# Ordering the stores of plain weights behind the TensorE instruction issued ahead of them

## The chip, the cores and the metric

The kernel runs on one core of a Trainium2 chip. The metric is the device time of one execution in microseconds (us); lower is better. The engines are TensorE (PE in the profile), VectorE (DVE), ScalarE (ACT), GpSimd (POOL) and SyncE (SP), which here does little but issue DMAs.

## The reference

Attention over pooled keys, then a gated feed-forward network, all in float32:

```
# q, k, v: (8 batches, 8 heads, 576 tokens, 64)
k_p = k.reshape(B, H, 72, 8, D).mean(axis=3)      # v_p likewise
scores = q @ k_p.T / sqrt(64)
attn = exp(scores - max) / (sum + 1e-9)
x = (attn @ v_p) -> 4608 tokens x 512
h = x @ w_in                                       # 512 x 2048
g = h * clip(h + 3, 0, 6) / 6
out = g @ w_out                                    # 2048 x 512
```

## The kernel before, in words

**Numbers.** A float32 operand is split into a high and a low part of TensorE's short type, and each product is made as high·high + high·low + low·high: three matmuls for one. `w_in` and `w_out` lie in SBUF as such pairs.

**Blocks of tokens.** The 4608 tokens are cut into blocks of 512, 256 and ten times 384. Blocks 0 to 3 are "plain". For each of 16 slices f of the hidden dimension a step makes h (L841, PE), relu (L849, ACT), the gate g (L853, DVE), its high part ghi (L857, ACT) and low part glo (L861, DVE); the second product out (L872, PE) follows two steps later. The finished sums go through ACT (L877) to DRAM by SP (L878). Blocks 4 to 11 are taken two at a time as four "super-blocks". There a 2x2 product is made of seven products of sums and differences (L1134 for the first matrix, L1188 and L1261 for the second), and the weights for these stream back from DRAM.

**Attention.** It goes in small pieces between the matmuls of the block ahead: loads of q, k and v (`qt` L241, `kst` L249, `vst` L284 and L288), scores (L463, PE), maximum (L467, DVE), exponential (L472, ACT), sums and reciprocals (`sm`, L489 and L490, DVE), scaling (`a`, L501, POOL), transposes (L572, L574, PE) with copies (L583, L585, L596, L598), and the product with v (L646, PE). The pooling of v is at L383 on DVE.

**Weights to DRAM.** During blocks 2 and 3, hooks that run after a step write what the super-blocks will stream:

- `sums_of` (L930 to L948), 16 rounds, at every even step of blocks 2 and 3: DVE adds two pairs of weight quarters into the tile `wq` (L939) and mixes them (L944, four times), ACT casts the high part (L945), DVE subtracts for the low part (L946), and SP stores four pieces of 128 KB (L948). The tile `wq` exists once, so a round's first addition must wait for the landing of the stores of the round before.
- `plain_of` and `store` (L950 to L962), 32 hooks with 56 stores of 256 KB in all (L951): weights as they are, straight from the tiles `w`, into the DRAM tensors `wd` (first matrix) and `w2d` (second). One hook follows each step of block 2, two follow each of the first eight steps of block 3.
- `swap`, after step 9 of block 3, gives half of the weight tiles back and opens the first pool of the weight stream; `chunk` (L980 to L994) then loads tiles of 512 KB (L992), four in the first pool (`wsFalse`) and three in the second (`wsTrue`). The second pool opens when block 3 ends. Its first tile lies where `wq` lay, so its load waits until the last round's four stores have landed.

**What sets the order.** Each engine has one queue and takes it in order; SP's queue holds every load and store. Up to step 3 of block 1 the order is a table written by hand (`ORDER`, applied by `put_in_order`). From there on a scheduler builds each engine's queue from the order of the source, its estimates, and the dependencies. `behind(ins, name)` (L166) adds one such dependency: the instruction stands behind the one named in the schedule. It adds no semaphore, so on the chip nothing waits for it. `traced` is the list of all instructions issued so far in the source. A DMA has one of eight semaphores in turn, so it also waits for the landing of the one eight before it.

Numbers behind an underscore are the program's names of buffers: `wq_3755`, `wq_3832` and `wq_3910` are the last three rounds of `sums_of`; `qt_1902` is a tile of q for block 2; `wsTrue_4002` is the first tile of the second weight pool.

Of the kernel before, what the change touches and what calls it, by code (L numbers as in the profile page):

```python
# [98 lines left out]
def attention_moe_kernel(  # L99
# [66 lines left out]
    def behind(ins, name):  # L166
        no_sync = mybir.DependencyInfo(mybir.DependencyClass.NoSync, mybir.DependencyReason.DATA)
        tc.add_manual_dep(ins, name, no_sync, reason="order")

    traced = nc.cur_bb.bb.instructions  # L170
# [778 lines left out]

    def store(to, src):  # L950
        nc.sync.dma_start(to, src)  # L951

    def plain_of(i, n):
        if n < 2:
            for o, (r, q) in list(RAW.items())[2 * n : 2 * n + 2]:
                store(dram_of(i, o), pair_of(i)[r][:, :, q])
        else:
            f = 2 * i + n - 2
            for m in range(2):
                w = w_of[f, 1][:, m].bitcast(F32).rearrange("p (q c) -> p q c", q=2)  # L960
                store(w2_dram[f // 4][:, f % 4, :, m], w)
# [605 lines left out]
```

## Time and profile before

| what | value |
|---|---|
| median of 3 runs | 894.1 us (892.81 to 894.3) |
| the profiled execution's own time | 893.88 us |
| its span, first to last instruction | 892.1 us |
| PE busy | 869.2 us, 97% of the span |
| DVE, ACT, POOL busy | 75%, 62%, 9% |
| granted TensorE clock | 1.00 throughout |
| DMA traffic | 200 MB, mean 224 GB/s |
| the chain of work that ended last | PE 80%, DVE 8%, DMA 5%, ACT 4% |

How to read the profile. A row of a timeline has the start, the length, the engine, the source line, the operation, output<-input, the shape and a count of instructions put together; in brackets stands the idle time of that engine ahead of the row and what ended it. A row of the windows has a stretch of time, and for each engine its busy time in it with its count of instructions; then the granted clock, the share of the DMA engines' time in use, and GB/s. "SPq" rows are issues of DMAs by SP; how long the transfer itself takes is told apart, as the time from issue to landing.

### The profile page before, as it was taken

The page shows a single profiled execution, that of the slowest core. Times are in us where ns is not written, and L with a number is a line of the kernel's source. Part 1 is how long each engine was busy: PE and PEld are TensorE (multiplying, and loading weights), DVE is VectorE, ACT ScalarE, POOL GpSimd, SP SyncE. Part 2 cuts the span into 40 slices and gives each one's busy share as a digit, 9 for nine tenths or more (in the row PEclk, how much of TensorE's full clock was granted, in tenths as well). Part 3 has the DMA queues.
Part 4 walks back from the last instruction along what each step waited for, and adds up shares of the span by engine and source line. Part 5 has one row for each costly group of instructions (what it writes and reads, how often), then busy time and mean ns, then how long its engine had stood idle before and what let it go on. Part 6 is the DMA issues. An engine that isn't in the chain of part 4 may idle for free.

```text
span 892.1 us, 15646 instructions
## 1 busy us (share of the span) xinstructions
PE 869.2 (97%) x5360; PEld 812.3 (91%) x5360; DVE 665.9 (75%) x1340; ACT 553.6 (62%) x1515; POOL 83.6 (9%) x168
## 2 busy tenths in 40 slices
PE   7899999999999999999999999999999999999998
PEld 6788888988989998998888999999999999999998
DVE  6999864567877785869788688897597877466664
ACT  5998766655656655778344688665577746355442
POOL 4100002110211100102000101100100200000000
PEclk9999999999999999999999999999999999999999
DMA  9970205995425234996587968877976777877873
GB/s 294 392 293 1 72 24 192 360 327 167 130 67 160 71 129 135 368 315 225 180 271 239 383 218 295 265 239 236 331 250 213 226 233 240 275 253 238 266 264 132
DMA packets 124654, 200.00 MB, mean 224 GB/s; under 512 B 13216, under 2 KB 81056, under 8 KB 124576
## 3 DMA queue, kind: packets, MB, share of 16 engines
q1 hardware_dynamic: 124432, 199.00, 67.8%
q8 instruction: 43, 0.70, 0.3%
q14 instruction: 35, 0.29, 0.1%
q10 hardware_dynamic: 144, 0.00, 0.0%
HBM read 158.08 MB, written 40.89 MB: 223 GB/s over the span
## 4 chain that ended last, share of the span: by engine, by line
PE 80%; DVE 8%; DMA 5%; ACT 4%; issue 2%; SPq 1%; POOL 0%; DVEq 0%; ACTq 0%; POOLq 0%
PE psx L1134 22%; PE psx L1261 19%; PE pso L872 12%; PE psh L841 12%; PE psx L1188 7%; PE psa L646 3%; PE psa L463 3%; ACT e L472 2%; PE psa L572 1%; DMA raw<-w_in_l 1%; DMA raw<-w_out_l 1%; DMA wd<-wq 1%; DVE vst L383 1%; DMA wsFalse<-wd 1%; DVE wq L939 1%
## 5 line engine op out<-in xcount | busy, mean ns | idle before, releaser
L1134 PE MATMUL psx<-x,wsFalse 128*128 128x384 f32 x768 | 151.8, 341 | 1.7 <-DVE g L1098 0.8
L841 PE MATMUL psh<-xhi,w 128*128 128x384 f32 (+2 forms) x520 | 145.9, 340 | 0.5 <-DVE g L853 0.4
L1134 PEld LDWEIGHTS psx<-x,wsFalse 128*128 128x128 f32 x768 | 133.6, 188 | 3.2 <-ACT c L1107 1.3
L1113 ACT CAST part<-g 128x768 fp32r<-128x768 f32 x100 | 83.3, 836 | 85.0 <-PE psx L1261 65.8
L1115 DVE TENSOR_TENSOR part<-g,part 128x768 fp32r<-128x768 f32 x100 | 95.2, 955 | 46.5 <-ACT part L1113 46.1
L872 PE MATMUL pso<-w,ghi 128*128 128x512 f32 x384 | 120.7, 398 | 0.4 <-ACT o L877 0.4
L1134 PE MATMUL psx<-x,wsTrue 128*128 128x384 f32 x576 | 115.8, 342 | 2.4 <-DMA wsTrue<-wd 2.3
L1261 PE MATMUL psx<-wsFalse,part 128*128 128x256 f32 x864 | 108.3, 282 | 1.5 <-DVE part L1115 1.1
L1261 PEld LDWEIGHTS psx<-wsFalse,part 128*128 128x128 f32 x864 | 105.2, 189 | 2.3 <-DVE part L1115 1.3
L1134 PEld LDWEIGHTS psx<-x,wsTrue 128*128 128x128 f32 x576 | 99.6, 188 | 3.1 <-DVE g L1092 3.1
L841 PEld LDWEIGHTS psh<-xhi,w 128*128 128x128 f32 x520 | 93.2, 188 | 8.2 <-DVE g L853 1.1
L472 ACT ACTIVATE e<-psa,mx 128x72 f32<-128x72 f32 x256 | 78.6, 324 | 23.7 <-DVE mx L467 22.4
L841 PE MATMUL psh<-xlo,w 128*128 128x384 f32 (+2 forms) x260 | 87.1, 336 | 0.0
L501 POOL TENSOR_TENSOR a<-e,sm 128x256 f32<-128x256 f32 x60 | 41.0, 683 | 478.3 <-DVE sm L490 377.9
L1261 PE MATMUL psx<-wsTrue,part 128*128 128x256 f32 x648 | 81.3, 283 | 0.0
L1261 PEld LDWEIGHTS psx<-wsTrue,part 128*128 128x128 f32 x648 | 79.3, 191 | 0.2 <-DVE part L1115 0.2
L872 PEld LDWEIGHTS pso<-w,ghi 128*128 128x128 f32 x384 | 69.1, 188 | 11.2 <-ACT o L877 0.7
L1090 ACT ACTIVATE r<-g,small 128x384 f32<-128x384 f32 x96 | 58.8, 621 | 28.4 <-DVE g L1098 28.0
L872 PE MATMUL pso<-w,glo 128*128 128x512 f32 x192 | 74.4, 399 | 0.0
L1098 DVE TENSOR_TENSOR g<-psx,c 128x384 f32<-128x384 f32 x96 | 52.3, 553 | 28.7 <-PE psx L1134 20.6
L1107 ACT COPY c<-psx 128x384 f32<-128x384 f32 x96 | 45.0, 485 | 28.5 <-PE psx L1134 28.1
L1092 DVE SCALAR_TENSOR_TENSOR g<-r,g 128x384 f32<-128x384 f32 x96 | 54.5, 576 | 9.7 <-ACT r L1090 9.2
(139 smaller groups left out, 1473.2 us busy)
## 6 DMA issues: line engine op xcount, KB each, us to landing
wsFalse<-wd SPq DMA_DIRECT2D x64, 512.0 KB, 4.6
wsTrue<-wd SPq DMA_DIRECT2D x48, 512.0 KB, 4.9
wsFalse<-w2d SPq DMA_DIRECT2D x31, 512.0 KB, 5.0
wsFalse<-w2t SPq DMA_DIRECT2D x27, 512.0 KB, 5.0
wsTrue<-w2d SPq DMA_DIRECT2D x21, 512.0 KB, 5.0
wsTrue<-w2t SPq DMA_DIRECT2D x21, 512.0 KB, 4.9
raw<-w_in_l SPq DMA_DIRECT2D x16, 512.0 KB, 8.6
raw<-w_out_l SPq DMA_DIRECT2D x16, 512.0 KB, 9.2
```

The costliest lines, as they stand in the source:

```text
L472: nc.scalar.activation(self.e[:, h], self.ps[:, h], AF.Exp, bias=self.mx[:, h : h + 1], accum_out=self.sm[:, h : h + 1])
L841: nc.tensor.matmul(self.ps, l[f][:, c, :], r[:, c, :], start=c == 0 and i == 0, stop=c == NCC - 1 and i == 2)
L872: nc.tensor.matmul(pos, l, r, start=f == 0 and i == 0, stop=f == NF - 1 and i == 2)
L1090: nc.scalar.activation(r, src, AF.Relu, bias=half_low, scale=GSCALE / (6.0 * WSCALE))
L1092: nc.vector.scalar_tensor_tensor(out=g_of[i][:, k], in0=r, scalar=GSCALE, in1=src, op0=ALU.min, op1=ALU.mult)
L1098: nc.vector.tensor_tensor(out=g_of[i][:, k], in0=ps, in1=kept, op=ALU.add)
L1107: nc.scalar.copy(c, ps)
L1113: nc.scalar.copy(t[:, 0], src)
L1115: nc.vector.tensor_tensor(out=t[:, 1], in0=src, in1=t[:, 0].bitcast(F32), op=ALU.subtract)
L1134: nc.tensor.matmul(ps, w[:, l, c * P : (c + 1) * P], t[:, r, c], start=o in (1, 2, 5) and c == 0 and k == 0, stop=c == 1 and k == 2, skip_ ...
L1188: nc.tensor.matmul(to, l, w[:, qs, r], start=f == 0 and k == 0, stop=end and k == 2)
L1261: nc.tensor.matmul(to, t[:, l, k, i * P : (i + 1) * P], w[:, k, r], start=begin and k == 0 and y == 0 and i % 2 == 0, stop=m == NM - 1 and ...
```

## The change

One line is added to `store`, the function that issues the 56 plain stores:

```diff
     def store(to, src):
         nc.sync.dma_start(to, src)
+        behind(traced[-1], next(i for i in reversed(traced) if i.engine == mybir.EngineType.PE).name)
```

Each store is placed behind the last PE instruction issued ahead of it in the source: as a rule an `out` matmul (L872) of the step whose hook it is, in a block's first two steps, which have none, a matmul of h (L841). As this enters a schedule, it moves rows on every engine. Lines behind L952 have numbers higher by one after it (L992 becomes L993).

The order is the same on each engine up to about the 610th row of PE, in block 1, and again from the second half of the first super-block. Three places in between matter.

**SP, at the end of block 1.** `wd` and `w2d` are the DRAM tensors of plain weights, `w_...` tiles of weights. Before, from the last early load of k to the load of qt_1902 (rows left out at the line of dots):

```order
L249 DMA kst_1647<-k_l 128x576
L951 DMA wd0_92<-w_0_344 128x2x256 x2
L951 DMA wd5_97<-w_1_486 128x2x256
L951 DMA w2d0_120<-w_0_431 128x2x256 x2
L241 DMA qt_1837<-q_l 128x4x128
...
L951 DMA wd22_114<-w_11_1049 128x2x256
L951 DMA w2d2_122<-w_10_1006 128x2x256 x2
L241 DMA qt_1902<-q_l 128x4x128
L951 DMA w2d2_122<-w_11_1049 128x2x256 x2
```

After, from the same load of k:

```order
L249 DMA kst_1647<-k_l 128x576
L241 DMA qt_1837<-q_l 128x4x128
L284 DMA vst_1839<-v_l 128x2x256
L284 DMA vst_1861<-v_l 128x2x256
L284 DMA vst_1904<-v_l 128x2x256
L284 DMA vst_1957<-v_l 128x2x256
L241 DMA qt_1902<-q_l 128x4x128
L241 DMA qt_2026<-q_l 128x4x128
L288 DMA vst_2028<-vr_l 32x2x256 x3
L249 DMA kst_2032<-k_l 128x576
L241 DMA qt_2450<-q_l 128x4x64
L951 DMA wd0_92<-w_0_344 128x2x256 x2
```

The loads of q, v and k for block 2 have moved ahead of the first plain store; the stores follow later, among other rows.

**DVE, the last rounds of `sums_of`, at the end of block 3.** `g` and `glo` are the steps' gate and low part, `mx` and `sm` the softmax's. Before:

```order
L946 TENSOR_TENSOR wq_3755<-wq_3755 128x512
L861 TENSOR_TENSOR glo_3821<-g_3816,ghi_3819 128x384
L853 SCALAR_TENSOR_TENSOR g_3861<-g_3861,psh_3848 128x384
L861 TENSOR_TENSOR glo_3866<-g_3861,ghi_3864 128x384
L939 TENSOR_TENSOR wq_3832<-w_14_1196 128x256
L939 TENSOR_TENSOR wq_3832<-w_15_1212 128x256
L853 SCALAR_TENSOR_TENSOR g_3894<-g_3894,psh_3881 128x384
...
L946 TENSOR_TENSOR wq_3832<-wq_3832 128x512
L853 SCALAR_TENSOR_TENSOR g_3942<-g_3942,psh_3929 128x384
L861 TENSOR_TENSOR glo_3947<-g_3942,ghi_3945 128x384
L467 TENSOR_REDUCE mx_4011<-psa_4013 128x4
L467 TENSOR_REDUCE mx_4038<-psa_4040 128x4
L939 TENSOR_TENSOR wq_3910<-w_14_1196 128x256
```

After:

```order
L853 SCALAR_TENSOR_TENSOR g_3894<-g_3894,psh_3881 128x384
L946 TENSOR_TENSOR wq_3755<-wq_3755 128x512
L861 TENSOR_TENSOR glo_3899<-g_3894,ghi_3897 128x384
L853 SCALAR_TENSOR_TENSOR g_3942<-g_3942,psh_3929 128x384
L939 TENSOR_TENSOR wq_3832<-w_14_1196 128x256
L939 TENSOR_TENSOR wq_3832<-w_15_1212 128x256
L861 TENSOR_TENSOR glo_3947<-g_3942,ghi_3945 128x384
...
L490 RECIPROCAL sm_4012<-sm_4012 128x4
L946 TENSOR_TENSOR wq_3832<-wq_3832 128x512
L939 TENSOR_TENSOR wq_3910<-w_14_1196 128x256
L939 TENSOR_TENSOR wq_3910<-w_15_1212 128x256
L944 TENSOR_TENSOR wq_3910<-wq_3910 128x128 x4
L946 TENSOR_TENSOR wq_3910<-wq_3910 128x512
```

Each round has moved back against the steps' gates: L946 of wq_3755 stood behind the gate g_3816 and now stands behind g_3894, two steps later, and the first additions of wq_3910 now stand directly behind L946 of wq_3832.

**SP, at the same place.** `out` are finished results, `ws` tiles of the weight stream. Before:

```order
L878 DMA out<-o_3977 128x512
L948 DMA wd27_119<-wq_3910 128x2x128
L948 DMA wd26_118<-wq_3910 128x2x128
L948 DMA wd25_117<-wq_3910 128x2x128 x2
L878 DMA out<-o_3983 128x512
L878 DMA out<-o_3989 128x512
L992 DMA wsFalse_4101<-wd7_99 128x1024
L992 DMA wsTrue_4002<-wd4_96 128x1024
```

After:

```order
L878 DMA out<-o_3977 128x512
L878 DMA out<-o_3983 128x512
L878 DMA out<-o_3989 128x512
L993 DMA wsFalse_4101<-wd7_99 128x1024
L948 DMA wd27_119<-wq_3910 128x2x128
L948 DMA wd26_118<-wq_3910 128x2x128
L948 DMA wd25_117<-wq_3910 128x2x128 x2
L993 DMA wsTrue_4002<-wd4_96 128x1024
```

The last round's stores stand behind two more outputs and a load of the weight stream, and directly ahead of the load that waits for them.

## The prediction

> **What bounds the kernel now.** I read the page first: is there one engine that everything waits for?
>
> ```profile
> span 892.1 us, 15646 instructions
> PE 869.2 (97%) x5360; PEld 812.3 (91%) x5360; DVE 665.9 (75%) x1340; ACT 553.6 (62%) x1515; POOL 83.6 (9%) x168
> ```
>
> TensorE (PE) works for 869.2 of 892.1 us. The change adds no arithmetic, so it can only touch the 23 us in which PE stands idle, or make new idle time. The profiled run took 893.88 us, its span and 1.78 us around it. My sum is made on 893.88; the median of the three runs shown is 894.1, 0.2 us higher, which I neglect. A measurement of this kernel tells about 0.2% from no change, 1.8 us; faster means below 892.1, slower above 895.7.
>
> Next, the instruction that is edited: the source view of L951, the plain stores.
>
> ```profile
> L951 SPq DMA_DIRECT2D w2d<-w x32: 428/724/1452, 149.9 to 198.1; - x32
> L951 SPq DMA_DIRECT2D wd<-w x24: 426/720/1174, 148.1 to 192.5; - x24
> its engine sat idle before it (us, times) until:
> who waited for it (us, times):
> busy tenths in 40 slices 0000000000000000000000000000000000000000
> DMA to landing us min/median/max: 3.0/4.7/6.6
> ```
>
> All 56 stores leave SP's queue as one burst between 148.1 and 198.7 us, and the list of who waited for them is empty: when they land is of no interest to anybody. What matters is what stands behind them and what is reordered around them. The order of the changed kernel agrees with before's on every engine up to about 178 us and again from about 450 us, so I read only that stretch: PE's idle time by windows, then each engine's timeline where a window has some.
>
> ```profile
> core 0: us, PE busy (x) PEld busy (x) DVE busy (x) ACT busy (x) POOL busy (x), PEclk, DMA share, GB/s
> 186.00:203.00 17.00, 15.39 (x85) 13.29 (x83) 10.58 (x30) 8.24 (x33) 2.35 (x5) 1.00 1.00 320
> 203.00:345.00 142.00, 141.30 (x759) 128.46 (x760) 108.46 (x273) 83.06 (x260) 15.80 (x29) 1.00 0.40 115
> 358.00:450.00 92.00, 89.99 (x507) 84.22 (x508) 74.23 (x175) 62.79 (x201) 12.13 (x24) 1.00 0.79 267
> 450.00:892.10 442.10, 434.44 (x2958) 422.28 (x2957) 324.67 (x568) 251.75 (x610) 26.78 (x52) 1.00 0.77 254
> ```
>
> PE misses 1.61 us in 186–203, 0.70 in 203–345, 2.01 in 358–450 and 7.66 in the common tail; the DMA engines are full (share 1.00) in the first of these. The granted clock is 1.00 in every row.
>
> **Part 1, removed: the crowd at 190–203 us.** Six rows of PE, with SP's, DVE's and ACT's row that lead to them:
>
> ```profile
> 183.54 0.55 SPq L241 DMA_DIRECT2D qt<-q_l  x1
> ...
> 191.09 0.46 DVE L467 TENSOR_REDUCE mx<-psa 128x4 f32<-128x288 f32 x1 [4.29 <-PE psa L463]
> ...
> 191.64 0.32 ACT L472 ACTIVATE e<-psa,mx 128x72 f32<-128x72 f32 x1 [5.64 <-DVE mx L467]
> ...
> 193.06 0.41 PE L572 MATMUL psa<-ident,a 128*128 128x128 f32 x2 [0.19 <-issue]
> 194.28 0.44 PE L572 MATMUL psa<-ident,a 128*128 128x128 f32 x2 [0.70 <-POOL a L501]
> 198.08 0.44 PE L646 MATMUL psa<-ahi,vhi 128*128 128x384 f32 x1 [0.25 <-DVE alo L585]
> 198.54 0.34 PE L646 MATMUL psa<-ahi,vlo 128*128 128x384 f32 x1
> 198.98 0.44 PE L841 MATMUL psh<-xhi,w 128*128 128x384 f32 x1
> 202.95 0.74 PE L872 MATMUL pso<-w,ghi 128*128 128x512 f32 x2 [0.36 <-ACT o L877]
> ```
>
> The load of qt_1902 stands behind 40 of the stores and leaves at 183.54. Its scores are therefore late; DVE sits idle for 4.29 us and ACT for 5.64 before them, and then scores, softmax, transposes and the first steps of block 2 all come at once. PE breaks five times: 0.19, 0.70, 0.25, 0.10 (198.98 less the end of the matmul before, 198.54 + 0.34) and 0.36, together 1.60 us, which is the window's 1.61. A break costs a little more than its idle row says, because matmuls overlap. I take that from the 36 in a row at 349.87 (quoted below): 6.50 us less one matmul's 0.34, over 35, is a pitch of 0.176, so a matmul of 0.34 hides 0.16 under its neighbour. Five times 0.16 is 0.8, and the crowd costs 2.4 us.
>
> In the changed order qt_1837, four vst, qt_1902 and qt_2026 come ahead of all 56 stores in SP's queue, and PE takes the scores of qt_1902 inside step 14 of block 1, before 186 us. DVE's and ACT's idle stretches get filled, and the crowd is gone. I put the saving at **2.4** us; at least 0, since ACT's part of the last break (an output's copy, 0.36) doesn't hang on the load, and other work may crowd instead.
>
> **Part 2, removed: two small breaks.**
>
> ```profile
> 248.04 0.35 PE L646 MATMUL psa<-ahi,vhi 128*128 128x192 f32 x1 [0.31 <-DVE alo L585]
> ...
> 256.54 0.44 PE L841 MATMUL psh<-xhi,w 128*128 128x384 f32 x1 [0.39 <-DVE g L853]
> ```
>
> These two are all of the 0.70 us of 203–345; with 0.16 each they cost 1.0. In the changed order DVE does no sums (L939) between the low halves that the first waits for. I take half, **0.5**, with 0 and 1.0 as ends. The stores themselves now lie between 187 and about 300 us, in a stretch with a DMA share of 0.40; nobody waits for their landing, so I charge nothing. The first reader, the weight stream's first tiles, comes at about 318 us, and without that cover each store would cost its 4.7 us of landing once.
>
> **Part 3, moved: the sums of weights at the end of block 3.** The tile wq exists once, so a round of it is a ring through three queues: DVE L939, L944, ACT L945, DVE L946, four stores on SP, their landing, then the next round's L939. DVE's waits for a landing (9.8 us in 7 times) and the ring's last two rounds:
>
> ```profile
> DVE wq L939 <- DMA wd<-wq: 9.8, 7, 3.3
> ...
> 338.09 0.55 DVE L853 SCALAR_TENSOR_TENSOR g<-g,psh 128x384 f32<-128x384 f32 x1 [1.09 <-ACT g L849]
> ...
> 340.86 0.69 DVE L946 TENSOR_TENSOR wq<-wq 128x512 fp32r<-128x512 f32 x1 [0.69 <-ACT wq L945]
> 342.34 0.55 DVE L853 SCALAR_TENSOR_TENSOR g<-g,psh 128x384 f32<-128x384 f32 x1 [0.79 <-ACT g L849]
> ...
> 345.12 0.76 DVE L939 TENSOR_TENSOR wq<-w 128x256 f32<-128x256 f32 x2 [0.35 <-DMA wd<-wq]
> ...
> 346.37 1.25 DVE L944 TENSOR_TENSOR wq<-wq 128x128 f32<-128x128 f32 x3
> 348.35 0.69 DVE L946 TENSOR_TENSOR wq<-wq 128x512 fp32r<-128x512 f32 x1 [0.73 <-ACT wq L945]
> ...
> 347.70 0.62 ACT L945 CAST wq<-wq 128x512 fp32r<-128x512 f32 x1 [1.89 <-issue]
> ...
> 341.58 1.96 SPq L948 DMA_DIRECT2D wd<-wq  x4
> 349.52 2.00 SPq L948 DMA_DIRECT2D wd<-wq  x4
> 352.64 0.40 SPq L992 DMA_DIRECT2D wsFalse<-wd  x1
> 353.22 0.82 SPq L992 DMA_DIRECT2D wsTrue<-wd  x2
> ...
> 353.22 5.34 DMA wsTrue<-wd
> ...
> 349.87 6.50 PE L1134 MATMUL psx<-x,wsFalse 128*128 128x384 f32 x36
> 358.70 1.47 PE L1134 MATMUL psx<-x,wsTrue 128*128 128x384 f32 x7 [2.34 <-DMA wsTrue<-wd]
> ```
>
> From issue of a round's first store to the next L939 it is 345.12 − 341.58 = 3.5 us. The first load of the second weight pool, wsTrue_4002, takes the place of wq in SBUF, so SP holds it until the last round's stores have landed: 349.52 + 3.5 = 353.0, issue 353.22, 5.34 us on the way, and PE stands for 2.34 before 358.70. So **this ring already sets the end of block 3**; every us by which it gets later, PE gets later.
>
> In the changed order the ring runs up to two steps of the block behind. Followed in before's clock: L946 of wq_3755 stands behind the g at 338.09, so it ends at 338.09 + 0.55 + 0.69 = 339.3; its stores have landed 3.5 later, at 342.8. L939 of wq_3832 stands behind the g at 342.34 (before: ahead of 338.09), so from 342.9. To the end of L946 of wq_3832 its own work and what stands between (glo, two mx, sm) are about 0.76 + 0.55 + 0.81 + 1.25 + 0.62 + 0.69 = 4.7, so 347.6. Stores, landing: 351.1, where L946 waits for nothing else. Then L939 of wq_3910: 0.76 + 1.25 + 0.62 + 0.69 with 0.1 of handover is 3.4, so 354.5 for the stores (before 349.52, **5.0 later**). The three outputs and wsFalse_4101, ahead of them now, are due by 352.64 and don't hold them. Landing 358.0, issue of wsTrue_4002 358.2.
>
> ```profile
> wsTrue<-wd SPq DMA_DIRECT2D x48, 512.0 KB, 4.9
> ```
>
> With the median of 4.9 it lands at 363.1, and PE goes on 0.13 later (358.70 − 353.22 − 5.34 = 0.14). One group of six matmuls, psx_3999<-x7_3958, has moved from ahead of this wait to behind it: 6 × 0.176 = 1.05. PE's place that was reached at 358.70 is reached at 363.2 + 1.05 = 364.3: **5.5 us later**. Ends: if the next L939 is held only by the four stores' issue (2.0) instead of 3.5, twice, it is 2.5; with the 5.34 us of the first load and 1.5 more of DVE's other work it is 7.5. What stands behind DVE's wait for the landing at 351.1 is the first group's g (L1098, L1099 after); PE's next groups wait for it and for ACT's copies behind L945, but only until about 357, inside the wait that is there anyway.
>
> [...]
>
> **Sum.** 893.88 − 2.4 − 0.5 + 5.5 = 896.5; the tail is ordered as before.
>
> **The rivals.**
>
> *The pause is paid back (no change).* While PE waits 5.5 us, DVE, ACT and SP go ahead with attention work that PE later stands for: 2.01 us in 358–450. Speaks for it: those waits are for that work. Against: DVE is itself held up at 351–355. If all come back: 896.5 − 2.0 = 894.5. Chance 0.28.
>
> *The ring is no later (faster).* The one place is the landing of wq_3910's stores. If the rounds catch up because L939 of wq_3832 and of wq_3910 find their landings done, wsTrue_4002 leaves as at 353.2 and only the moved group is paid: 893.88 − 2.9 + 1.05 = 892.0, and 890.5 with the second part whole and the group hidden. It decides at a landing of wsTrue_4002 at 358.7 in before's clock. Against it: L939 of wq_3910 stands directly behind L946 of wq_3832 and needs its landing, with 3.5 us between. [...] Chance 0.13.
>
> *A new crowd on top (slower still).* Behind the late ring DVE has L1098's, the part sums and vst pooling of the first super-block, all 5 us late; if PE must stand for them once more by 2–3 us, 899. Chance 0.09.
>
> *It does nothing.* The added line is an order only, with no semaphore; the changed order moves hundreds of rows, so: 893.9, chance 0.01.
>
> **How the numbers follow.** The forecast's own case has 0.49, with 894.5 to 898.5 from the ends of part 3 beside the full gains. Faster is the second rival, 0.13; the same holds the first rival, the last one, and a little of the forecast's lower end, 0.32; slower is the rest, 0.55. For 8 in 10 the range reaches into the faster case, to 891.3, and into the crowd, to 899.3.
>
> **What would show it.** Right: L951 from about 187 to 300 us; DVE's 4.29 and ACT's 5.64 gone and 186–203 with PE idle under 0.4; the last L948 issued about 5 us later, relative to PE, and PE's row at wsTrue with 7 us of idle or near it. Wrong: wsTrue_4002's wait still at 2.3, or breaks elsewhere in 203–345 over 1 us.

## The result, and the profile after

The changed kernel takes 906.37 us (median of 4 runs, 904.69 to 908.16), before on the same chip 893.45 (891.7 to 894.3). The ratio is 1.0147, 95% interval 1.0122 to 1.0173: slower by 12.9 us, where 2.6 were forecast. The profiled execution took 908.16 us, 14.28 more than the profiled one of before. Of the runs below, one execution of e10 (2714 us) and one of e11 (954 us) lie far above their fellows and are left out of the ratios.

Page of after, the first line and the engines' busy time:

```profile
span 906.3 us, 15649 instructions
PE 876.4 (97%) x5360; PEld 818.3 (90%) x5360; DVE 665.5 (73%) x1340; ACT 555.1 (61%) x1515; POOL 83.4 (9%) x168
```

PE does the same 5360 matmuls in 7.2 us more of busy time, which a later order can't do by waiting alone: part of the loss is a slower clock (0.83 and 0.74 granted in two of the windows below). The source view of L951, the stores of plain weights:

```profile
L951 SPq DMA_DIRECT2D w2d<-w x32: 359/542/1188, 188.2 to 300.9; - x32
L951 SPq DMA_DIRECT2D wd<-w x24: 434/508/765, 186.5 to 298.1; - x24
who waited for it (us, times):
```

They lie where they were forecast, and still nobody is named as waiting for them. Windows of after, then of before (its rows for 186–203 and 203–345 stand in the prediction):

```profile
186.00:203.00 17.00, 17.00 (x95) 16.09 (x94) 10.79 (x31) 8.67 (x26) 1.15 (x3) 1.00 0.54 170
203.00:300.00 97.00, 96.66 (x532) 87.54 (x530) 70.23 (x195) 57.96 (x207) 13.61 (x27) 1.00 0.75 232
300.00:345.00 45.00, 42.25 (x213) 37.88 (x214) 35.17 (x76) 24.22 (x55) 0.99 (x2) 1.00 0.39 122
345.00:365.00 20.00, 15.16 (x67) 14.14 (x66) 8.27 (x20) 8.42 (x23) 2.18 (x4) 0.83 0.72 235
365.00:420.00 55.00, 55.00 (x334) 54.41 (x333) 45.69 (x110) 44.82 (x155) 9.06 (x18) 1.00 0.90 297
420.00:440.00 20.00, 15.43 (x62) 13.14 (x61) 15.11 (x41) 9.00 (x31) 2.97 (x4) 0.74 0.43 137
```

```profile
300.00:345.00 45.00, 45.00 (x233) 40.82 (x232) 35.03 (x73) 24.06 (x52) 1.85 (x4) 1.00 0.34 106
345.00:365.00 20.00, 17.66 (x102) 16.85 (x101) 11.31 (x28) 12.16 (x34) 1.78 (x4) 1.00 0.78 259
365.00:420.00 55.00, 53.93 (x328) 53.07 (x327) 45.62 (x117) 44.13 (x156) 8.55 (x18) 1.00 0.89 301
420.00:440.00 20.00, 19.76 (x100) 16.57 (x100) 15.37 (x35) 10.73 (x33) 3.58 (x6) 1.00 0.54 171
```

PE is without a break in 186–203 now. It loses in three places: 2.75 us of idle time in 300–345; 4.84 in 345–365, where before has 2.34, with a granted clock of 0.83; and 4.57 in 420–440, before 0.24, at 0.74. Matmul by matmul, after stands to before (in before's clock) so:

| place in before, us | 180 | 300 | 331 | 345 | 364 | 378 | 423 | 499 | end |
|---|---|---|---|---|---|---|---|---|---|
| after later by, us | -1.7 | -5.0 | -1.6 | -1.5 | +4.5 | +4.5 | +10.2 | +12.2 | +14.3 |

The -1.7 at 180 and the +2.1 behind 499 lie where the two orders are the same; I take them for the scatter of single executions. What lies between is 13.9, and the difference of the medians is 12.9.

**300–345.** Timeline rows of after, PE, DVE and SP:

```profile
301.15 0.41 PE L646 MATMUL psa<-ahi,vhi 128*128 128x384 f32 x1 [1.19 <-ACT ghi L857]
324.57 0.44 PE L841 MATMUL psh<-xhi,w 128*128 128x384 f32 x1 [1.22 <-DVE g L853]
...
298.62 0.76 DVE L939 TENSOR_TENSOR wq<-w 128x256 f32<-128x256 f32 x2 [1.61 <-DMA wd<-wq]
316.34 0.76 DVE L939 TENSOR_TENSOR wq<-w 128x256 f32<-128x256 f32 x2 [1.97 <-DMA wd<-wq]
323.97 0.55 DVE L853 SCALAR_TENSOR_TENSOR g<-g,psh 128x384 f32<-128x384 f32 x1
...
284.93 2.66 SPq L951 DMA_DIRECT2D w2d<-w  x4
293.67 2.06 SPq L948 DMA_DIRECT2D wd<-wq  x4
298.61 3.00 SPq L951 DMA_DIRECT2D w2d<-w  x4
```

The stores of block 3 now stand between the rounds of `wq` in SP's queue. DVE waits longer for the landing of a round, and the gates that PE needs (g, L853) are queued behind that wait. At 324 they are not directly behind it: from the end of the wait at 316.34 to the gate at 323.97 DVE works without a pause, mostly on the super-block's sums (L1039 and L1047, seven rows). DVE's list of waits in 200–345, of after, has 17.1 us in 11 waits for that landing; the same list of before has 9.4 in 6.

```profile
DVE wq L939 <- DMA wd<-wq: 17.1, 11, 3.3
```

**The end of block 3.** Timeline rows of after:

```profile
353.15 4.97 PE L1135 MATMUL psx<-x,wsFalse 128*128 128x384 f32 x18 [2.42 <-ACT c L1108]
360.55 1.94 PE L1135 MATMUL psx<-x,wsTrue 128*128 128x384 f32 x6 [2.42 <-DMA wsTrue<-wd]
...
349.96 0.76 DVE L939 TENSOR_TENSOR wq<-w 128x256 f32<-128x256 f32 x2 [3.61 <-DMA wd<-wq]
...
352.10 0.62 ACT L945 CAST wq<-wq 128x512 fp32r<-128x512 f32 x1 [3.42 <-DVE wq L944]
352.63 0.47 ACT L1108 COPY c<-psx 128x384 f32<-128x384 f32 x1
...
353.47 1.98 SPq L948 DMA_DIRECT2D wd<-wq  x4
357.05 0.81 SPq L993 DMA_DIRECT2D wsTrue<-wd  x2
```

The last round's stores leave at 353.47 (before 349.52) and the load of wsTrue at 357.05 (353.22). PE stands twice, not once: first for the copy c, which is queued on ACT behind the cast of the late round, then for wsTrue.

**420–440.** Timeline rows, then the loads of the pooled tile in the tile view of vst, 415–424, all of after:

```profile
424.03 1.32 PE L1135 MATMUL psx<-x,wsTrue 128*128 128x384 f32 x6 [2.42 <-DVE g L1099]
426.71 1.33 PE L463 MATMUL psa<-kbd,qt 128*128 128x144 f32 x4 [1.36 <-DVE arem L598]
431.40 2.29 PE L1135 MATMUL psx<-x,wsTrue 128*128 128x384 f32 x6 [0.79 <-DVE g L1099]
...
422.82 0.69 DVE L383 TENSOR_TENSOR vst<-vst 96x512 f32<-96x512 f32 x1 [3.71 <-DMA wsFalse<-w2d]
423.43 0.55 DVE L1099 TENSOR_TENSOR g<-psx,c 128x384 f32<-128x384 f32 x1
...
414.12 1.75 SPq L993 DMA_DIRECT2D wsFalse<-w2d  x2
415.96 1.32 SPq L288 DMA_DIRECT2D vst<-vr_l  x3
```

```profile
L288 SPq DMA_DIRECT2D vst<-vr_l x3: 382/418/418, 416.0 to 416.9; - x3
DMA to landing us min/median/max: 5.7/6.0/6.1
```

The bracket names a load of wsFalse, which the pooling L383 doesn't read; by their times it is the three loads of vr, issued up to 416.9 and landed 5.7 later, at 422.6. They stand behind two loads of 512 KB in SP's queue; in before the same three leave ahead of those two (410.83 against 412.72). While DVE waits 3.71 us at the pooling, the gate behind it (L1099) stands still, and PE for it.

**The clock.** Windows of after, cut at the edges of its stretches of half clock, then two of before, cut in steps of the same 3.41 us from the first record of its clock (6.16 us), PE alone:

```profile
350.69:354.10 3.41, 0.99 (x6) 1.00 0.73 244
354.10:357.51 3.41, 3.41 (x13) 0.50 0.56 154
357.51:360.93 3.42, 1.00 (x6) 1.00 0.82 283
360.93:364.34 3.41, 3.41 (x13) 0.50 1.00 331
425.78:436.02 10.24, 8.52 (x25) 0.50 0.45 130
```

```profile
354.32:357.73 3.41, 2.04 (x12) 1.00 0.91 329
357.73:361.15 3.42, 2.45 (x14) 1.00 1.08 367
```

Behind the breaks PE runs at a granted clock of 0.50. If half of its busy time there is lost, an estimate from that figure, it is (3.41 + 3.41) x 0.50 = 3.4 us at the end of block 3, and 8.52 x 0.50 = 4.3 at 426–436. The matmuls say a little less: those of 128x384 start 0.320 us apart in the first stretch (354.47 to 357.35), and 0.173 ahead of the break (349.87 to 350.39), by which it would be 3.1 and 3.9. In before the only break of that size, 2.34 us, leaves the clock at 1.00. Of its idle time 1.37 us lie in the first of the two rows and 0.97 in the second; in after 2.42 lie in one row, twice.

### The profile page after: what moved, and what is told of

It is laid out like the page before. It is cut to its first block, busy times and chain, and to the rows that moved or that the text cites. A ratio compares the mean times of both kernels' runs of the same rounds, so it can differ in the third digit from the quotient of the medians.

```text
span 906.3 us, 15649 instructions
## 1 busy us (share of the span) xinstructions
PE 876.4 (97%) x5360; PEld 818.3 (90%) x5360; DVE 665.5 (73%) x1340; ACT 555.1 (61%) x1515; POOL 83.4 (9%) x168
## 4 chain that ended last, share of the span: by engine, by line
PE 52%; DVE 6%; DMA 4%; ACT 2%; issue 1%; SPq 1%; DVEq 0%; ACTq 0%
PE psx L1135 22%; PE psx L1262 18%; PE psx L1189 7%; PE psa L463 2%; PE psa L646 2%; DMA wd<-wq 1%; DMA qt<-q_l 1%; SPq L948 1%; PE psa L572 1%; DVE x L1039 1%; DVE g L1093 1%; DMA wsFalse<-wd 1%; DMA wsFalse<-w2d 1%; DVE vst L383 1%; DVE wq L946 0%
## 5 line engine op out<-in xcount | busy, mean ns | idle before, releaser
L1135 PE MATMUL psx<-x,wsFalse 128*128 128x384 f32 x768 | 155.5, 345 | 4.3 <-ACT c L1108 3.0
L841 PE MATMUL psh<-xhi,w 128*128 128x384 f32 (+2 forms) x520 | 146.7, 341 | 1.9 <-DVE g L853 1.8
L1135 PEld LDWEIGHTS psx<-x,wsFalse 128*128 128x128 f32 x768 | 136.0, 191 | 6.0 <-ACT c L1108 4.0
L1135 PE MATMUL psx<-x,wsTrue 128*128 128x384 f32 x576 | 119.2, 347 | 5.7 <-DVE g L1099 3.2
L872 PE MATMUL pso<-w,ghi 128*128 128x512 f32 x384 | 119.6, 398 | 0.0
L1135 PEld LDWEIGHTS psx<-x,wsTrue 128*128 128x128 f32 x576 | 101.7, 192 | 7.4 <-DVE g L1099 4.0
L841 PEld LDWEIGHTS psh<-xhi,w 128*128 128x128 f32 x520 | 93.1, 188 | 10.3 <-DVE g L853 3.4
L841 PE MATMUL psh<-xlo,w 128*128 128x384 f32 (+2 forms) x260 | 87.0, 335 | 0.0
L872 PEld LDWEIGHTS pso<-w,ghi 128*128 128x128 f32 x384 | 69.0, 188 | 10.5
L1099 DVE TENSOR_TENSOR g<-psx,c 128x384 f32<-128x384 f32 x96 | 52.0, 552 | 29.4 <-PE psx L1135 21.7
L872 PE MATMUL pso<-w,glo 128*128 128x512 f32 x192 | 73.3, 396 | 0.0
L1093 DVE SCALAR_TENSOR_TENSOR g<-r,g 128x384 f32<-128x384 f32 x96 | 55.0, 582 | 11.7 <-ACT r L1091 11.3
```

The source lines that it names most:

```text
L841: nc.tensor.matmul(self.ps, l[f][:, c, :], r[:, c, :], start=c == 0 and i == 0, stop=c == NCC - 1 and i == 2)
L872: nc.tensor.matmul(pos, l, r, start=f == 0 and i == 0, stop=f == NF - 1 and i == 2)
L1093: nc.vector.scalar_tensor_tensor(out=g_of[i][:, k], in0=r, scalar=GSCALE, in1=src, op0=ALU.min, op1=ALU.mult)
L1099: nc.vector.tensor_tensor(out=g_of[i][:, k], in0=ps, in1=kept, op=ALU.add)
L1135: nc.tensor.matmul(ps, w[:, l, c * P : (c + 1) * P], t[:, r, c], start=o in (1, 2, 5) and c == 0 and k == 0, stop=c == 1 and k == 2, skip_ ...
```

## The experiments

Two kinds of edit are used. One changes `store` or a tile. The other, a graft, takes before's source and hangs every engine's instructions one behind the other in an order written out as numbers:

```diff
     if ORDER:
         put_in_order()
+    graft()
```

`graft` calls `behind` for each row of its table GRAFT; with after's whole order in it, it gives after's queues. Below, `after[:1440]` stands for the first 1440 rows of an engine in after, `before[1440:]` for the rest in before. The lines of grafted kernels have higher numbers: L1157 is L939, L1166 is L948, L1071 is L853, L1352 is L1134, L803 is L585. All kernels compute the whole reference.

| run | us, median | ratio to before on the same chip, 95% interval |
|---|---|---|
| e1_after_to_block3 | 914.82 | 1.0238 (1.0208 to 1.0267) |
| e2_after_to_super | 897.85 | 1.0047 (1.0029 to 1.0066) |
| e3_after_part_first | 907.5 | 1.0136 (1.0096 to 1.0176) |
| e4_before_part_first | 892.47 | 0.9984 (0.9970 to 0.9999) |
| e5_after_one_row | 903.6 | 1.0110 (1.0090 to 1.0130) |
| e6_front_only | 900.24 | 1.0080 (1.0064 to 1.0097) |
| e7_no_pause | 906.24 | 1.0141 (1.0120 to 1.0163) |
| e8_front_and_early_load | 902.0 | 1.0094 (1.0077 to 1.0111) |
| e9_block2_stores_only | 894.23 | 1.0004 (0.9988 to 1.0021) |
| e10_block3_stores_only | 903.57 | 1.0114 (1.0084 to 1.0143) |
| e11_front_stores_early | 906.18 | 1.0142 (1.0115 to 1.0168) |
| e12_after_stores_early | 910.34 | 1.0189 (1.0161 to 1.0218) |
| e13_block2_stores_before_rest | 893.04 | 0.9997 (0.9982 to 1.0012) |
| e14_block2_front_after_rest | 901.93 | 1.0093 (1.0059 to 1.0127) |

### Which stretch of the order costs what

**e1 and e2** take after's order for all that the source issues ahead of block 3 (e1) or ahead of the first super-block (e2), and before's for the rest.

```diff
+GRAFT = {engine: after[:block_3] + before[block_3:]}            # e1
+GRAFT = {engine: after[:super_block_1] + before[super_block_1:]} # e2
```

> Every engine has the changed kernel's order for what is issued up to the end of block 2, and before's order from block 3 on (imposed by a table). Theory A, all of the loss is made from block 3 on, by the late ring of wq and what follows from it: only the gains of the crowd at 190-203 us and of the small breaks are left, so 2.5 to 3.5 us below before, about 890.5. Rival B, the reordered loads and stores of block 2 also cost later, since loads for block 3's attention now stand behind a late burst of stores: 893 to 896.

> The changed kernel's order for all that is issued up to the end of block 3, before's order from the first super-block on. The two orders differ in that part up to about 435 us. Theory A, the loss of 6.7 us at 420-436 us in the changed kernel is made by its own order there (DVE takes the pooling of the last v rows, which waits for a late load, ahead of two gates): it falls away and the time is 6 to 7 us below the changed kernel's, about 900. Rival B, it is made by the pause at the end of block 3, after which all loads come late by the same amount, whatever the order: 905 to 907, the changed kernel's own time.

e1 says nothing: at its seam a load of q came to stand behind stores that themselves wait for later rows, and PE stood 20.8 us at 297.86. e2 keeps after's breaks of block 3 (1.35 at 302.53, 1.19 at 325.91, 2.44 at 354.51, 3.01 at 361.96), and of the loss at 420–440 little is left. Its window, PE alone, beside which after has 30.43 of 35 at a clock of 0.85 and before 33.69 at 1.00:

```profile
405.00:440.00 35.00, 32.98 (x190) 1.00 0.60 188
```

e2 is 8.5 us faster than after. So the loss at 420–440 goes with the order of the first super-block, not with what comes ahead of it.

**e5** is after with two DVE rows moved: the poolings at 422.82 and 423.97 behind the two steps of gates, L1099 and L1093, that stood behind them.

```diff
 DVE:
-L383 vst, L1099 g, L489 sm, L383 vst, L585 alo, L490 sm, L1093 g
+L1099 g, L489 sm, L585 alo, L490 sm, L1093 g, L383 vst, L383 vst
```

> The changed kernel's order on every engine but for one place on DVE: the pooling of the last v rows (L383, vst_4864 with vst_4923, two additions), which waits 3.7 us for its load, stands behind the gates of g6_4777 (two rows of L1099 and L1093) instead of ahead of them. Theory A, that one wait with PE's next groups queued behind it makes the loss at 420-436 us and the half clock there: the stretch falls from 9.3 us over its pitch to 3 to 5, the time to 900 to 902. Rival B, the loss comes from many rows of that stretch or from late loads in general: 904 to 907.

Its median is 2.8 us under after's, though the two intervals overlap. In the profile the first break in 424–432 goes, but PE then waits 2.48 for the next copy (arem, L598) behind the same poolings; its idle time in 405–440 is 3.39 us, where after has 4.57, and its granted clock there 0.95, where after has 0.85. The row is a part of the 420–440 loss, not all of it.

**e6 and e7** put the seam ahead of the last rounds of `wq`. e6 has before's order from there; e7 has, besides, after's order again from the first super-block.

```diff
+GRAFT = {PE: after[:1440] + before[1440:], DVE: after[:494] + before[494:], ACT: after[:480] + before[480:],
+         POOL: after[:103] + before[103:], SP: after[:213] + before[213:]}   # e6; e7: then after from the super-block
```

> A better seam than the first splice: the changed kernel's order up to about 300 us (on SP through the stores of the round wq_3547, with all 56 plain stores as late as in the changed kernel), before's order behind that. Theory A, the change's gains are real and its loss is made wholly behind this place: 2.5 to 3.5 us under before, about 890.5. Rival B, loads behind the spread stores cost what the crowd gave: 893 to 895.

> As the run before it up to the first super-block (so without the late ring and the pause at the end of block 3), then the changed kernel's own order from the first super-block on. Theory A, the loss at 420-436 us is the order's own: 6 us on top of the run before it, about 896.5. Rival B, that order only loses when all loads have been put off by the pause: about 890.5 to 892, the same as the run before it.

Timeline rows of e6 (L1169 is the plain store):

```profile
302.03 0.66 PE L790 MATMUL psa<-ident,a 128*128 128x128 f32 x2 [4.97 <-DVE alo L803]
...
300.79 0.76 DVE L1157 TENSOR_TENSOR wq<-w 128x256 f32<-128x256 f32 x2 [4.97 <-DMA wd<-wq]
...
286.86 2.58 SPq L1169 DMA_DIRECT2D w2d<-w  x4
292.32 2.46 SPq L1169 DMA_DIRECT2D w2d<-w  x3
295.85 1.96 SPq L1166 DMA_DIRECT2D wd<-wq  x4
```

Before's order wants the next round's additions early; with the stores ahead of them the round's own stores leave at 295.85, and DVE and PE stand 4.97 us. After's order has the rounds later, and its breaks here are smaller. e7 loses at 420–440 like after (a break of 2.45 at 428.80, 1.36 at 431.47), but it also has 4.37 at 301.67 and 3.71 at 363.98, so it doesn't separate order and late arrival by itself.

### Which stores

**e9** and **e10** apply the edit to the first 28 stores (block 2) or the last 28 (block 3), and leave the rest to the scheduler.

```diff
         nc.sync.dma_start(to, src)
+        n_stored[0] += 1
+        if n_stored[0] <= 28:      # e9; in e10: > 28
+            behind(traced[-1], next(i for i in reversed(traced) if i.engine == mybir.EngineType.PE).name)
```

> The added line acts on the first 28 stores alone (those of block 2); the 28 of block 3 are left as before, and the scheduler sets them ahead of the rounds of block 3. Theory T, the loss starts where the second 28 stores stand between the rounds of wq on SP and in the DMA engines at 280-302 us, and the ring is late from there on: without them the ring keeps its place, the front's gain stays, and the time is 1 to 4 us under before, 889.5 to 892.5. Rival O, any new order of these blocks upsets later places by chance: over 896.

> The added line acts on the last 28 stores alone (those of block 3). Theory T: the ring is late as in the changed kernel, with DVE's waits for a landing of wq well over before's 9.4 us in 200-345 us and a break before the first use of wsTrue, so slower than before by 8 to 15 us, 901 to 908, and, if the first 28 stores still hold the loads up, without the front's gain. Rival O: no tie to which half is moved, so near 897.

Timeline rows of e9, then of e10:

```profile
337.09 10.04 SPq L948 DMA_DIRECT2D wd<-wq  x8
348.86 0.88 SPq L997 DMA_DIRECT2D wsTrue<-wd  x2
...
353.17 3.39 PE L1139 MATMUL psx<-x,wsTrue 128*128 128x384 f32 x18 [0.58 <-DMA wsTrue<-wd]
```

```profile
352.49 1.99 SPq L948 DMA_DIRECT2D wd<-wq  x4
356.08 0.81 SPq L997 DMA_DIRECT2D wsTrue<-wd  x2
...
352.17 4.98 PE L1139 MATMUL psx<-x,wsFalse 128*128 128x384 f32 x18 [3.21 <-ACT c L1112]
```

With block 2's stores alone the ring is done at 347.1, earlier than in before, PE waits 0.58 us for wsTrue, and 180–350 has no break over 0.3. With block 3's alone the ring is as late as in after, and the breaks of 3.21 and 2.26 us are back, with a granted clock of 0.86 in 345–370 (after 0.86, before 1.00). So most of the loss hangs on block 3's 28 stores: e10 is 10.2 us slower than its before, after 12.9. e9 has no gain either. Matmul by matmul its lead on before grows from 0.3 us at 180 to 5.6 at 415 and is 2.2 at 437: PE stands 2.52 us at 416.72, for DVE behind the same kind of pooling, with a clock of 0.55 behind it, in 417–420.

**e13 and e14** have e9's front on every engine up to the end of block 3, then before's order (e13) or after's (e14).

```diff
+GRAFT = {PE: e9[:1740] + before[1740:], DVE: e9[:590] + before[590:], ACT: e9[:551] + before[551:],
+         POOL: e9[:106] + before[106:], SP: e9[:247] + before[247:]}   # e13; e14: + after[...]
```

> Only block 2's first 28 stores stand behind TensorE, as in the run that did that alone, and from the end of block 3 on every engine has before's order. Theory (what block 2's moved stores win before 300 us is real, some 3 us, and was lost at 412 to 418 us by the order that the plan makes of that stretch): 889.5 to 891.5 us, the break at the partial of wsTrue stays under 1 us, and 400 to 420 us loses what before loses there. Rival (TensorE that comes early at the super-block waits there for its loads whatever the order is): 893 to 894.5 us, with 2 to 3 us more idle time than before between 345 and 440 us.

> The same front, and after's order from the end of block 3 on, so that TensorE comes to 353 us without the two breaks of after. Theory (the loss at 420 to 436 us is the order's own: a mask of VectorE that waits for the landing of vr stands ahead of two gates): 420 to 436 us loses 7 to 9 us as in after, 896 to 900 us in all. Rival (that loss comes from the late arrival, or from the half clock that the breaks at 353 and 361 us leave): under 4 us is lost there, 889 to 893 us.

e13 is not faster than before, as its rival said. That what the front wins is given back in the super-block is shown in e9, at 416.72 and for e9's own order; in e13 it is not shown, since its profiled execution took 898.82 us, the longest of its 12 runs, and stands for none of the others. e14, whose front has no break up to 345 us, loses in the first super-block again: 5.5 us of idle time in 345–370 and 4.5 in 405–440, at clocks of 0.93 and 0.95. But its breaks at 352 and 360 (1.90 and 3.50, for loads of wsTrue and wsFalse) didn't go, so my condition for it, a front that arrives without breaks, holds only up to 350 us. With e2 the four medians make a square:

| front \ first super-block | before's order | after's order | difference |
|---|---|---|---|
| block 2's stores alone | 893.04 (e13) | 901.93 (e14) | 8.9 |
| all stores | 897.85 (e2) | 906.37 (after) | 8.5 |
| difference | 4.8 | 4.4 | |

The two causes add up, 4.8 + 8.9 against 13.3 in all, as far as can be told (e14's interval alone is 3 us to each side): block 3's stores in the front, and the order that the scheduler made of the first super-block.

The idle time of PE in 405–440, over all the profiles, says the same of the second. It is 4.5 to 5.2 us in the five kernels with after's order there (after, e3, e7, e12, e14), whatever comes ahead, and 1.3 to 2.7 in the eight with before's (before, e1, e2, e4, e6, e8, e11, e13). What differs with the front is the granted clock of the same stretch: 0.85 in after and e3, 0.88 in e12, 0.95 in e7 and e14.

### Can it be mended?

**e3** is after, **e4** before, with the pool's tiles laid out so that the first load of wsTrue isn't where `wq` was.

```diff
+    late[1].tile([P, 2, 2, HALF], F32R, name="part", bufs=3)
```

> The changed kernel, its order unchanged, with the second pool's tile part allocated ahead of wsTrue, so that wsTrue no longer lies where wq lay: its load needs no landing of wq's last stores, but still stands behind their issue in SP's queue. Theory A, the wait for that landing is worth the 1.6 us between the last store's issue and wsTrue's, and the half clock after it: wsTrue leaves at 355.5 instead of 357.05, PE's second break is 0.8 or less instead of 2.42, and the time 1.5 to 3.5 us lower than the changed kernel's, 903 to 905. Rival B, with less of a pause the clock stays up and the loss at 420-436 us goes too: under 900. Rival C, nothing, since the first break (a copy on ACT behind the last cast of wq) alone sets it: 906.

> The kernel before, its order unchanged, with the same move of wsTrue off the place of wq. Theory A of the prediction, the landing of wq's last stores sets PE's 2.34 us at 358.70: wsTrue leaves at its turn in SP's queue. Since wsFalse leaves ahead of it at 352.64 for a reason of its own (a tile that PE still reads), only 0 to 0.3 us can be gained by that: 893 to 894. Rival B, the row at 353.22 waited for the landing and all else was free from 351.6: 1.5 us gained, 892.

In before the break of 2.34 falls to 1.59, and the time by 0.16% (0.01 to 0.30), the lowest of all, at the edge of what can be told. In after it gains nothing that can be told: the break at wsTrue is 1.89 instead of 2.42, and that for the copy c stays 2.45. So the tile's place is worth 0.5 to 0.8 us of PE's wait; it is not what costs the 6 at the end of block 3.

**e8** is e6 with that layout and the two loads of wsTrue right behind the stores of wq_3910 in SP's queue.

```diff
 SP: L948 wd<-wq_3910 x4
+SP: L992 wsTrue_4002, wsTrue_4004
```

> The front as in the run with the better seam, before's order behind it, wsTrue moved off the place of wq, and the first two loads of wsTrue put directly behind the last round's four stores on SP, ahead of two outputs and of wsFalse, which waits for PE. They should leave at about 351.6 less the front's 3 us instead of 353.2, and PE's 2.3 us there shrink to 0.5 to 1. With both gains 888 to 889; if the load's way through the full DMA engines takes longer by as much, 890.5.

The wait for wsTrue goes (0.53 is left), but a load of q is late instead (1.02 at 366.20), an a at 391.79 (1.92, with a clock of 0.95 over 370–405), and 3.75 at 301.08 stays. Its median is 1.8 us above e6's, with overlapping intervals: nothing is gained.

**e11 and e12** are e6 and after with block 3's 28 stores moved up, four behind each of the first seven rounds of `wq`.

```diff
 SP: L948 wd<-wq (round r of block 2) x4
+SP: L951, four of block 3's stores
```

> As the run with the better seam (the changed kernel's order up to 300 us, before's behind), but on SP the 28 stores of block 3 are moved up, four behind each of the first seven rounds' stores of block 2. Theory T: that run's break of 5 us at 302 us was a round waiting for stores queued behind these; it goes, and with it what followed, so 889.5 to 892. Rival: twice as many stores in block 2 hold its rounds up in the same way: 894 to 900.

> The changed kernel's order on every engine, but on SP the 28 stores of block 3 moved up in the same way. Theory T: DVE's waits for a landing of wq in 200-345 us fall from 17.1 us to 10 or less, PE's break at 301 us goes, those at 324 and 329 shrink; but DVE's order still has the last rounds late, so the two breaks at the end of block 3 and the loss at 420-436 us stay: 902.5 to 905. Rival P, the late ring is the waits' doing alone and the order adds nothing: under 898.

e11 is slower than e6, and e12 no faster than after. e12 loses the break at 301 and those at 324 and 329 (0.34 at 335 is left), as it would if block 3's stores had made them, but PE stands 3.69 us at 215.19 (e11 3.62 at 214.23). In e11 DVE waits there 3.40 us for loads of vr, which SP issues at 210.17 in the middle of the stores. In both places the stores stand between rounds of `wq` and loads that are soon needed; the burst of before is over at 198.7, the first round's stores leave behind it, from 204.2.

## Why the prediction was too small, point by point

By the table of matmuls, in before's places:

| stretch, us | forecast | came |
|---|---|---|
| 180–300, the crowd and the small breaks | -2.9 | -3.3 |
| 300–345, behind block 3's stores | 0 | +3.5 |
| 345–364, the ring at the end of block 3 | +5.5 | +6.0 |
| 364–499, the first super-block | 0 | +7.7 |
| together | +2.6 | +13.9 |

The steps that failed are the two zeros.

**The crowd and the two small breaks: right.** But the runs with that gain and no loss behind it in the front (e9, e13) end within 0.2% of before: the gain is not kept. That was in no term of the sum.

**"Nobody waits for their landing, so I charge nothing": the first step that failed.** It looked at the landing of the stores and not at what stands behind them in SP's queue. The view of waits can't show it: DVE waits for the stores of `wq`, which carry another name. In 300–345 it cost 3.5 us, of which 2.75 are idle time in three breaks, and the prediction had itself named breaks there over 1 us as what would show it wrong. In after the list of who waits for these stores is still empty: what was lost came by waits for other transfers.

**The ring at the end of block 3: right in size, not in its parts.** It is not one wait of 7 us at wsTrue, but two of 2.42 and an estimated 3.4 us of half clock, where before has one of 2.34: 2.5 + 3.4 = 5.9. "Only inside the wait that is there anyway" was wrong for the copies behind L945: they made a wait of their own. So the size is in part luck: the half clock, which the sum did not have, stands for the wait that did not come. Two numbers of the working are off besides. A round of the ring has four mixes (L944), and the 1.25 us that the sum takes for them is the row of three. And 894.5, the lower end of its own case, does not come out of its terms: 893.88 − 2.9 + 2.5 is 893.5.

**"The tail is ordered as before", and a new crowd at 2 to 3 us with a chance of 0.09: the larger miss.** The order differs to about 450 us, and I followed it no further than 364. The scheduler put two loads of 512 KB ahead of those of vr; the place lost 7.7 us (4.5 to 12.2 in the table): 4.3 of idle time in 420–440 (4.57 less 0.24) and an estimated 4.3 of half clock, less the 1.07 that before loses in 365–420. By the square of medians after's order from there is worth 8.5 to 8.9. The rival had the right place and mechanism (DVE's part sums, pooling of vst, PE standing for them once more), but a third of the price.

**"The pause is paid back", 0.28: wrong.** Between 364 and 378 nothing comes back. PE does run without a break in 365–420, where before loses 1.07 us, but only to stand longer at 424. DVE and ACT didn't win from PE's pause, since the same ring held them (3.61 and 3.42 us in the rows above).

**"The granted clock is 1.00 in every row": true of before, and not of after.** Half clock costs an estimated 7.7 us (3.4 + 4.3; 7.0 by the matmuls' distance) in after's profiled execution, which no term and no bound contained.

What is open: how much of the 420–440 loss would be left if PE came there without any earlier break. Its idle time there is 4.5 to 5.2 us in the five kernels named above, however PE comes; the granted clock is not the same (0.85 to 0.95). e14 was to tell, and had breaks of its own at 352 and 360.

## What to carry to other kernels

An empty list of waiters for a DMA says nothing of what it costs the transfers behind it in its queue (that of L951 is empty in before and in after, 12.9 us apart): before moving stores, look for short rings (a tile that exists once, stored and refilled) on the same queue, and for the in-order engine that waits for them with other engines' work behind it. A line that only changes a schedule must be followed to the last row that differs, and each place where a wait for a load has moved ahead of a gate priced at a load's whole time. Where an engine is 97% busy, time won ahead of a stretch that is set by loads may not be kept (here it was not, in e9 and e13). And a break can cost more than its own time: behind each of two of 2.42 us PE ran 3.41 us at a clock of 0.50 in after, an estimated 1.7 us more each time.

## What the runs showed of the hardware

The granted clock fell to half behind some breaks of about 2 us, and not behind others of the same length. In after it is 0.50 from 354.10 to 357.51, from 360.93 to 364.34 and from 425.78 to 436.02, stretches of 3.41, 3.41 and 10.24 us, and all six edges lie whole multiples of 3.41 us apart. Before has no such stretch between 6.16 us and the end of its span. The table has the mean granted clock of a stretch that holds a break or lies behind it:

| run | break, us | stretch, us | granted clock |
|---|---|---|---|
| before | 2.34 at 358.7 | 345–370 | 1.00 |
| e4 | 1.59 at 356.7 | 345–370 | 1.00 |
| e2 | 2.44 at 354.5 | 354–361 | 1.00 |
| e2 | 3.01 at 362.0 | 361–367 | 0.72 |
| after | 2.42 at 353.2 | 354.10–357.51 | 0.50 |
| after | 2.42 at 360.6 | 360.93–364.34 | 0.50 |
| e10 | 3.21 at 352.2, 2.26 at 359.4 | 345–370 | 0.86 |
| e8 | 1.92 at 391.8 | 370–405 | 0.95 |
| e11 | 3.62 at 214.2 | 214–218 | 0.50 |

The length of a break alone doesn't tell: e8 lost clock with one of 1.92 us, its longest in 370–405, and e2 lost none in 354–361 behind one of 2.44. Before's 2.34 us lie in two rows of 3.41 us, after's 2.42 in one row each time (the rows under "The clock"), so that before's full clock may have been luck; that is a guess from two profiles, and no run was made to show it. One stretch of 3.41 us costs up to an estimated 3.41 x 0.50 = 1.7 us, and executions of one kernel differ in clock: the 19 of before beside e1 to e4 have means from 0.996 to 1.000, and one such stretch is 0.002.
